# The beginning of a fused Fourier-mixing and feed-forward kernel: bit conversion without ScalarE, more buffers, spare PSUM banks, a shorter second chunk

## The chip, the cores and the metric

One Trainium2 chip; the program runs on one of its cores. The metric is the device time of one execution in microseconds (us), as a median of several executions. A profile is one more execution under the hardware profiler. TensorE multiplies matrices, VectorE and ScalarE do elementwise work, GpSimd does it too, slower here (a product of 128x512 elements took 1.30 us on it and 0.69 on VectorE), SP (SyncE) only issues DMAs. Runs whose time lies over 1.5% above the fastest of the same kernel count as slow.

## The reference

For x of (8, 3008, 256) the kernel computes a real FFT over the 3008 positions, multiplies by a complex filter, transforms back, and sends the 24064 resulting rows through a feed-forward block with a hard-swish:

```python
X = np.fft.rfft(x, axis=1)
F = (filt_r + 1j * filt_i)[None, :, :]
y = np.fft.irfft(X * F, n=x.shape[1], axis=1).astype(np.float32)
h = y.reshape(24064, 256) @ w_in            # (256, 2048), float64
g = h * np.clip(h + 3.0, 0.0, 6.0) / 6.0
out = (g @ w_out).astype(np.float32)        # (2048, 256), float64
```

The two weight matrices come as float64. The kernel has to turn their bits into float32 itself.

## The kernel before

The transform is split as 3008 = 47 x 64. For each batch: *first forward stage* (`a_unit`, eight units of four columns, results stored to z in DRAM), *second forward stage* (z loaded again, `b_unit` for 12 pairs of frequencies, filter product `f_unit` and `y_unit` on VectorE, inverse `bi_unit`, stored to g), *last stage* (`n_unit` on chunks of five of the 32 column groups, 94 tokens each). The main loop then runs the feed-forward block over 47 blocks of 512 tokens, eight items to a block. Batches 1 to 7 are transformed inside that loop; batch 0 has to be done ahead of it, and while that happens the weights are converted. That beginning is what the change is about.

```python
    def w_conv(i):                                    # 512 KB of float64 bits to float32
        ...
        v.tensor_scalar(out=big, in0=hi, ... shift left 3, and)
        v.scalar_tensor_tensor(out=big, in0=hi, scalar=top_c, in1=big, and, or)
        high = hi.bitcast(FP32)
        nc.scalar.activation(out=high, in_=high, func=AXT.Abs)
        v.tensor_scalar(out=rest, in0=big, ... exponent)
        v.tensor_scalar(out=lo, in0=lo, ... low bits as a fraction)
        v.scalar_tensor_tensor(out=rest, ...)         # low part
        v.scalar_tensor_tensor(out=rest, ...)         # plus high part
        v.tensor_scalar(out=high, in0=high, scalar1=SMALL, scalar2=None, op0=ALU.is_ge)
        nc.gpsimd.tensor_tensor(out=w_part(i)[1], in0=two(rest), in1=two(high), op=ALU.mult)
        # ... four sums or differences of 128x128 on GpSimd
    def a_unit(b, c):
        xc = xs[(b * NB + c) % 3]                     # three buffers for x
        t = t1p.tile(...)                             # two buffers
        ps = [psF.tile([P, 2, D], FP32, name="psf", tag="f") for h in range(2)]   # two banks
        # ... 4 matmuls, then two ScalarE evictions into t
    # the beginning of batch 0
        for c in range(3):
            x_load(0, c)
        w_load(0)
        w_load(1)
        for c in range(NB):                           # NB = 8
            a_unit(0, c)
            z_store(0, c, (nc.sync, nc.scalar))       # 2 DMAs on each queue
            if c + 3 < NB:
                x_load(0, c + 3)
            elif c + 3 == NB:
                table_load(0, 0)
            if c % 2:
                convert(1)
        # ... z loads and tables, then for i in range(NU + 1):  (NU = 12)
                b_unit(0, i); f_unit(0, i); y_unit(0, i)
                if i % 3 == 1:
                    convert(1)
                # ... bi_unit(0, i - 1), g_store, the next loads
        convert(2)
        # ... last-stage loads, n_unit for two chunks, main loop with the other six conversions
```

## Time and profile before

| | before |
|---|---|
| median | 2829.74 us (2827.22 to 2830.05) |
| span of the profiled run | 2827.1 us |
| first z load issued | 50.6 us |
| VectorE's first filter product | 58.4 us |
| its last y | ends at 121.9 us |
| first product of the main loop | 144.5 us |

The times of the table are starts and ends read in the timeline. TensorE is full from about 215 us to the end, so only the beginning can change, and in it the questions are which engine, queue or wait sets each of its stages. The prediction below shows the lines.

### The profile page before, as it was taken

What the parts mean: (1) busy time and instruction counts of PE and PEld (TensorE: products, weight loads), DVE (VectorE), ACT (ScalarE), POOL (GpSimd) and SP (SyncE); (2) the same over time, 40 slices, a digit from 0 to 9 for tenths busy, and PEclk for the clock granted to TensorE, in tenths of its full rate; (3) what the DMA queues carried; (4) which work ended last, traced back from release to release, by engine and by line L of the source; (5) the groups of instructions that cost most, each with busy time, mean ns of one, the idle gap of its engine ahead of it and who ended that gap; (6) DMA issues with size and microseconds to landing.
All of it is one profiled execution on the core that took longest, in us unless ns stands there. A gap on an engine that the chain in (4) does not pass through costs nothing.

```text
span 2827.1 us, 47246 instructions
## 1 busy us (share of the span) xinstructions
PE 2728.8 (97%) x18096; PEld 2467.2 (87%) x18096; DVE 1981.8 (70%) x3463; ACT 1340.4 (47%) x2686; POOL 411.1 (15%) x604
## 2 busy tenths in 40 slices
PE   4589999999999999999999999999999999999997
PEld 1369988999889998899989999899998999999996
DVE  4777875777657776577766777667775677766665
ACT  2144445444554445544455444544455444445443
POOL 3361012100120011201021101210012100000000
PEclk9799999999999999999999999999999999999998
DMA  7543213321233112322124221342113421100000
GB/s 211 174 128 111 78 55 100 94 64 53 76 84 103 57 60 71 93 84 81 40 81 112 62 66 42 87 115 76 48 47 90 112 66 47 40 26 24 17 8 16
DMA packets 127673, 211.89 MB, mean 75 GB/s; under 512 B 22232, under 2 KB 86360, under 8 KB 127448
## 3 DMA queue, kind: packets, MB, share of 16 engines
q1 hardware_dynamic: 104216, 151.69, 19.0%
q0 software_dynamic: 19104, 52.46, 6.4%
q10 hardware_dynamic: 4128, 4.72, 0.5%
q8 instruction: 143, 2.34, 0.3%
q14 instruction: 82, 0.67, 0.1%
HBM read 133.81 MB, written 74.97 MB: 74 GB/s over the span
## 4 chain that ended last, share of the span: by engine, by line
PE 92%; DVE 4%; DMA 2%; ACT 1%; issue 1%; POOL 0%; SPq 0%; POOLq 0%; ACTq 0%; DVEq 0%
PE po L418 41%; PE al L342 23%; PE be L342 17%; PE psn L317 4%; PE psf L261 3%; PE psf L289 3%; PE psf L236 2%; DMA z_tmp<-t 1%; DVE g L392 0%; DVE g L399 0%; DVE s L183 0%; DVE s L193 0%; DVE s L275 0%; DVE h L368 0%; DVE s L274 0%
## 5 line engine op out<-in xcount | busy, mean ns | idle before, releaser
L418 PEld LDWEIGHTS po<-w_out,g 128*128 128x128 f32 x10528 | 1401.8, 192 | 123.0 <-DVE g L400 30.4
L418 PE MATMUL po<-w_out,g 128*128 128x128 f32 x10528 | 1426.8, 276 | 4.6 <-DVE g L392 4.0
L392 DVE SCALAR_TENSOR_TENSOR g<-r,h 128x512 f32<-128x512 f32 x752 | 516.7, 687 | 256.5 <-ACT r L387 243.4
L387 ACT ACTIVATE r<-h,half_c 128x512 f32<-128x512 f32 x752 | 542.7, 722 | 321.1 <-DVE h L368 308.8
L342 PE MATMUL al<-xt,w_in 128*128 128x256 f32 x2256 | 676.1, 382 | 6.3 <-DVE h L373 4.7
L368 DVE TENSOR_TENSOR h<-be,s 128x512 f32<-128x512 f32 x376 | 259.6, 690 | 276.2 <-PE be L342 254.7
L342 PE MATMUL be<-xn,w_in 128*128 128x256 f32 x1504 | 447.8, 379 | 0.0
L342 PEld LDWEIGHTS al<-xt,w_in 128*128 128x128 f32 x2256 | 342.9, 192 | 9.7 <-DVE h L373 5.5
L382 ACT ACTIVATE h<-al 128x256 f32<-128x256 f32 x376 | 144.4, 384 | 373.6 <-PE al L342 373.6
L342 PEld LDWEIGHTS be<-xn,w_in 128*128 128x128 f32 x1504 | 286.1, 190 | 38.9
L373 DVE TENSOR_TENSOR h<-al,s 128x256 f32<-128x256 f32 x376 | 159.4, 424 | 191.6 <-PE al L342 191.2
L400 DVE TENSOR_TENSOR g<-g 128x512 f32<-128x512 f32 x376 | 261.4, 695 | 12.9
L363 ACT ACTIVATE s<-al 128x256 f32<-128x256 f32 x376 | 144.5, 384 | 202.0 <-PE al L342 202.0
L354 ACT ACTIVATE s<-be 128x256 f32<-128x256 f32 x376 | 144.4, 384 | 178.3 <-PE be L342 178.3
L342 PE MATMUL al<-xn,w_in 128*128 128x256 f32 x752 | 225.2, 381 | 0.5 <-ACT h L382 0.5
L342 PE MATMUL be<-xt,w_in 128*128 128x256 f32 x752 | 224.1, 380 | 0.0
L249 POOL DMA_DIRECT2D z_tmp<-t x224 | 132.5, 596 | 422.6 <-ACT t L239 419.5
L353 ACT ACTIVATE s<-al 128x256 f32<-128x256 f32 x376 | 144.4, 384 | 68.9 <-PE al L342 68.9
L399 DVE TENSOR_TENSOR g<-g 128x256 f32<-128x256 f32 x376 | 166.5, 443 | 12.8
L402 DVE TENSOR_TENSOR g<-g 128x256 f32<-128x256 f32 x376 | 165.0, 439 | 12.8
L342 PEld LDWEIGHTS be<-xt,w_in 128*128 128x128 f32 x752 | 143.2, 190 | 19.4
L317 PEld LDWEIGHTS psn<-wai,t 128*128 128x128 f32 x1024 | 135.4, 197 | 18.1 <-POOL w_out L202 12.5
(50 smaller groups left out, 1753.2 us busy)
## 6 DMA issues: line engine op xcount, KB each, us to landing
t<-z_tmp SPq DMA_DIRECT2D x48, 512.0 KB
t<-g_tmp SPq DMA_DIRECT2D x184, 120.0 KB
z_tmp<-t POOLq DMA_DIRECT2D x224, 96.0 KB, 2.8
g_tmp<-t POOLq DMA_DIRECT2D x42, 512.0 KB, 3.4
xs<-in_x_dram SPq DMA_DIRECT2D x128, 128.0 KB
out_dram<-o SPq DMA_DIRECT2D x328, 47.0 KB
ft<-in_filt_r_dram SPq DMA_DIRECT2D x96, 128.0 KB
ft<-in_filt_i_dram SPq DMA_DIRECT2D x96, 128.0 KB
```

The costliest lines, as they stand in the source:

```text
L317: nc.tensor.matmul(ps[:, ts(q, TOK)], t4[i % 2][:, q, ts(dh, P)], wai, start=True, stop=True)
L342: nc.tensor.matmul(ps, w_in[p][:, w, :], x, start=start, stop=stop, skip_group_check=True)
L353: nc.scalar.activation(out=s[:, 0, :], in_=al, func=AXT.Copy)
L363: nc.scalar.activation(out=s[:, 1, :], in_=al, func=AXT.Copy)
L368: nc.vector.tensor_tensor(out=st["h"][0].rearrange("p (a n) -> p a n", a=2), in0=be, in1=s, op=ALU.add)
L373: nc.vector.tensor_tensor(out=st["h"][1][:, 256:512], in0=al, in1=s5, op=ALU.add)
L387: nc.scalar.activation(out=r, in_=st["h"][i], func=AXT.Relu, bias=half_c, scale=1.0 / 6.0)
L392: nc.vector.scalar_tensor_tensor(out=st["g", k, p][:, o:o + 2, :].rearrange("p a n -> p (a n)"), in0=st["r", i], scalar=1.0, in1=st["h"][i ...
L399: v.tensor_tensor(out=g[:, G1, :], in0=g[:, G3, :], in1=g[:, G22, :], op=ALU.add)
L400: v.tensor_tensor(out=g[:, G3:G2 + 1:2, :], in0=g[:, G3:G1 + 1, :], in1=g[:, G11:G11 + 1, :].broadcast_to([P, 2, 256]), op=ALU.subtract)
L402: v.tensor_tensor(out=g[:, G4, :], in0=g[:, G12, :], in1=g[:, G2, :], op=ALU.subtract)
L418: nc.tensor.matmul(st["po", k][bank][:, part, u, :], g[:, a, ts(u, P)], w_out[p][:, w, :], start=(p == 0 and n in OPENS and u == 0), stop= ...
```

## The change

The intent: get batch 0 through its transform sooner. ScalarE's Abs leaves the conversion, so that evictions never queue behind a conversion, and the compare at its end moves from VectorE to GpSimd; six chunks of x have a place at once (three of them in `xn`, idle until the last stage) and are asked for on two queues; four tiles of bits instead of two can be in flight (two of them in the idle `g` buffers); six conversions stand beside the first stage; the forward stages of batch 0 use the four PSUM banks of the down product, idle until the main loop; and the second last-stage chunk has one column group instead of five, so that the main loop starts after six groups instead of ten.

```diff
     def w_load(i):
+        if i < 8 and i % 4 > 1:
+            t = gp.tile([P, 7, 256], FP32, name="g").bitcast(I32)[:, 0:4, :].rearrange(...)
+        else:
+            t = op.tile([P, 1024], I32, name="bits", tag="o")
...
-        high = hi.bitcast(FP32)
-        nc.scalar.activation(out=high, in_=high, func=AXT.Abs)
...
-        v.tensor_scalar(out=high, in0=high, scalar1=SMALL, scalar2=None, op0=ALU.is_ge)
+        v.tensor_scalar(out=hi, in0=hi, scalar1=20, scalar2=0x7FF,
+                        op0=ALU.logical_shift_right, op1=ALU.bitwise_and)
+        high = hi.bitcast(FP32)
+        nc.gpsimd.tensor_scalar(out=high, in0=hi, scalar1=897.0, scalar2=None, op0=ALU.is_ge)
         nc.gpsimd.tensor_tensor(out=w_part(i)[1], in0=two(rest), in1=two(high), op=ALU.mult)
...
+    def bank(b):
+        if b:
+            return psF.tile([P, 2, D], FP32, name="psf", tag="f")
+        st["bank"] = i = (st.get("bank", -1) + 1) % 4
+        return psO.tile([P, 2, 2, P], FP32, name="po%d" % i).rearrange("p a u m -> p a (u m)")
...
-    chunks = [(b, j, min(NJ, HC - j)) for b in range(B) for j in range(0, HC, NJ)]
+            n = 1 if b == 0 and j == NJ else min(NJ, HC - j)
...
-        for c in range(3):
-            x_load(0, c)
-        w_load(0)
-        w_load(1)
+        for c in range(6):
+            x_load(0, c, (nc.sync, nc.scalar)[c % 2])
...
+        convert(0)                    # loads every bits tile that has a free buffer
         for c in range(NB):
             a_unit(0, c)
             z_store(0, c, (nc.sync, nc.scalar))
-            if c + 3 < NB:
-                x_load(0, c + 3)
-            elif c + 3 == NB:
+            if c < 2:
+                x_load(0, c + 6)
+            if c == 2:
                 table_load(0, 0)
-            if c % 2:
-                convert(1)
+        convert(6)
...
-                if i % 3 == 1:
+                if i % 3 == 2 and i < NU - 1:
                     convert(1)
```

More of the change, by code (lines that the diff above doesn't have):

```diff
@@ L41 @@
 NJ = 5
-SMALL = float(np.array(897 << 20, np.int32).view(np.float32))
 RING = 3 * BLK
@@ L164, in w_part, with w_before @@
         return src.rearrange("(a p) d -> p a d", p=P), w_out[p][:, 0:4, :].rearrange("p (a j) m -> p a (j m)", a=2)
+    def w_before(i):
+        return i - 4 if i < 10 else i - 2
     def w_load(i):
-        if i >= NCONV:
-            return
-        t = op.tile([P, 1024], I32, name="bits", tag="o")
+        if i < 8 and i % 4 > 1:
+            t = gp.tile([P, 7, 256], FP32, name="g").bitcast(I32)[:, 0:4, :].rearrange("p a n -> p (a n)")
+        else:
+            t = op.tile([P, 1024], I32, name="bits", tag="o")
         nc.gpsimd.dma_start(t.rearrange("p (a d) -> p a d", a=2), w_part(i)[0])
@@ L173, in w_conv @@
     def w_conv(i):
-        if i >= NCONV:
-            return
         words = st.pop(("bits", i)).rearrange("p (n two) -> p n two", two=2)
@@ L217, with x_tile, x_load @@
     G11, G3, G1, G2, G4, G12, G22 = range(7)
-    def x_load(b, c):
-        t = xs[(b * NB + c) % 3]
+    def x_tile(b, c):
+        i = (b * NB + c) % 3
+        if b == 0 and 3 <= c < 6:
+            return xn.rearrange("p a n -> p (a n)")[:, ts(i, XC * D)].rearrange("p (j d) -> p j d", j=XC)
+        return xs[i]
+    def x_load(b, c, q=None):
+        q = q or nc.sync
+        t = x_tile(b, c)
         rows = x[b].rearrange("(a c) d -> a c d", c=NC)
@@ L225, in x_load @@
             for r, n in ((0, 32), (32, NA - 32)):
-                nc.sync.dma_start(t[h * 64 + r:h * 64 + r + n, :, :], rows[r:r + n, ds(h * HC + c * XC, XC), :])
+                q.dma_start(t[h * 64 + r:h * 64 + r + n, :, :], rows[r:r + n, ds(h * HC + c * XC, XC), :])
+    def bank(b):
[3 more added lines that the diff above has]
+        return psO.tile([P, 2, 2, P], FP32, name="po%d" % i).rearrange("p a u m -> p a (u m)")
     def a_unit(b, c):
-        xc = xs[(b * NB + c) % 3]
+        xc = x_tile(b, c)
         t = t1p.tile([P, 2, XC // 2, D], FP32, name="t1")
-        ps = [psF.tile([P, 2, D], FP32, name="psf", tag="f") for h in range(2)]
+        ps = [bank(b) for h in range(2)]
         for g in range(2):
@@ L258, in b_unit @@
         c, r = divmod(2 * i, TC)
-        ps = psF.tile([P, 2, D], FP32, name="psf", tag="f")
+        ps = bank(b)
         for u in range(2):
@@ L296, in g_store @@
         q.dma_start(g_d[b, ts(c, TC), :, :].rearrange("k p d -> p k d"), st.pop(("t3", b, c)))
-    chunks = [(b, j, min(NJ, HC - j)) for b in range(B) for j in range(0, HC, NJ)]
+    chunks = []
+    for b in range(B):
+        j = 0
+        while j < HC:
+            n = 1 if b == 0 and j == NJ else min(NJ, HC - j)
+            chunks.append((b, j, n))
+            j += n
     def token(i):
@@ L471 @@
     with tc.manual_schedule():
+        nc.sync.dma_start(wa, wa_d)
+        for t in xs[:2]:
+            nc.vector.memset(t, 0.0)
+        for t in xs[2], xn:
+            nc.gpsimd.memset(t, 0.0)
         nc.vector.memset(half_c, 0.5)
         nc.vector.memset(top_c, -0x40000000)
-        for i, t in enumerate(xs):
-            (nc.vector, nc.gpsimd, nc.vector)[i].memset(t, 0.0)
-        nc.sync.dma_start(wa, wa_d)
-        for c in range(3):
-            x_load(0, c)
-        w_load(0)
-        w_load(1)
-        done = 0
-        def convert(n):
-            nonlocal done
-            for _ in range(n):
-                w_conv(done)
-                w_load(done + 2)
-                done += 1
+        for c in range(6):
+            x_load(0, c, (nc.sync, nc.scalar)[c % 2])
+        loaded = done = 0
+        def convert(n):
+            nonlocal loaded, done
+            for i in range(n + 1):
+                while loaded < NCONV and w_before(loaded) < done:
+                    w_load(loaded)
+                    loaded += 1
+                if i < n:
+                    w_conv(done)
+                    done += 1
+        convert(0)
         for c in range(NB):
```

## The prediction

> **What bounds the kernel now.** I read the page first. Its slice rows say where time is left:
>
> ```profile
> PE   4589999999999999999999999999999999999997
> DVE  4777875777657776577766777667775677766665
> PEclk9799999999999999999999999999999999999998
> ...
> PE 92%; DVE 4%; DMA 2%; ACT 1%; issue 1%; POOL 0%; SPq 0%; POOLq 0%; ACTq 0%; DVEq 0%
> ```
>
> A slice is 70.7 us. From the fourth on TensorE is full to the end, and nothing in the diff touches that part except the cutting of batch 0 into last-stage chunks (same matmuls, one more chunk). PE is busy 2728.8 of 2827.1 us, so everything that is not PE work is 98 us, nearly all in the first 215 us, and it could not all be won: 2% of the time would be 57 us. So I cut the beginning into stages, by the busy-time view, at points found in the timeline: 0 to 50.6 the first forward stage (DFT over a, store of z); to 58.4 the first load of z until VectorE starts; to 121.9 the second forward stage, paced by unit; to 144.3 the tail (last g store, first last-stage matmuls); to 209.6 the seven items of the main loop that still hold conversions.
>
> ```profile
> core 0: us, PE busy (x) PEld busy (x) DVE busy (x) ACT busy (x) POOL busy (x), PEclk, DMA share, GB/s
> 0.00:50.60 50.60, 23.79 (x64) 4.84 (x64) 19.20 (x32) 12.61 (x21) 18.83 (x31) 1.00 0.69 197
> 50.60:58.40 7.80, 2.04 (x5) 1.70 (x6) 0.00 (x0) 0.00 (x0) 2.82 (x3) 1.00 0.84 257
> 58.40:121.90 63.50, 41.79 (x89) 25.07 (x87) 57.11 (x88) 8.80 (x15) 17.20 (x23) 0.85 0.60 180
> 121.90:144.30 22.40, 10.46 (x44) 9.62 (x44) 7.85 (x14) 3.62 (x6) 9.27 (x15) 0.50 0.74 194
> 144.30:209.60 65.30, 57.65 (x334) 42.33 (x333) 55.28 (x86) 30.89 (x63) 45.22 (x62) 0.95 0.44 126
> ```
>
> Stage one: no engine is half busy, and the DMA engines are at 0.69. The chain of waits of that stretch names what sets it (column: share of the chain): DMA of z, 48.9%.
>
> ```profile
> by line: DMA z_tmp<-t 48.9%; PE psf L236 13.0%; DMA xs<-in_x_dram 11.6%; DMA t<-z_tmp 10.0%; issue 4.9%; ACT t L239 4.2%; SPq L226 2.7%; DVE xs L479 1.6%; SPq L249 1.1%; ACTq L249 0.7%; DVE half_c L476 0.1%; SPq L254 0.1%; ACTq L239 0.1%; D
> ```
>
> Stage two: VectorE busy 57.11 of 63.50, so it is the bound. The remaining 6.4 us are short gaps. In the waits of 56 to 124 us two lines matter: VectorE waited for the second forward matmul 14.1 us, of which 11.4 are the stage's first load, so only 2.7 us within the stage; and the matmul of the inverse waited for ScalarE's eviction, because that eviction stood in ScalarE's order behind an Abs that waited for VectorE.
>
> ```profile
> ACT bits L187 <- DVE s L183: 34.4, 3, 20.3
> ...
> DVE s L273 <- PE psf L261: 14.1, 4, 11.4
> ...
> PE psf L289 <- ACT t L292: 9.1, 4, 2.8
> ```
>
> The tail: the timeline shows the last g store issued at 124.73, then
>
> ```profile
> 119.67 13.11 SPq L311 DMA_DIRECT2D t<-g_tmp  x16
> ...
> 135.89 8.82 PE L317 MATMUL psn<-wai,t 128*128 128x94 f32 x40 [11.82 <-POOL w_out L202]
> ```
>
> The reader is to see that these forty matmuls (20 in the program, two passes each) start when the last loads, which ended their issue at 132.8, can have landed; the wait is put down to GpSimd, but nothing these matmuls read comes from GpSimd's conversion, so I take it for the DMA. Each takes 0.22 us from start to start, at the half clock of that row.
>
> **What the Trainium skill says.** (1) "DMA: Bandwidth & Descriptors", Issuing engines are not separate DMA queues: DMAs of several issuers run on the same 16 engines and interleave, and a second issuer saves only issue time. The trace agrees in that sum: with all three issuers busy (50.6 to 58.4) the share is 0.84 at 257 GB/s. So x on ScalarE's queue is no new bandwidth. (2) "SBUF — State Buffer", SBUF: two separate sides: a VectorE instruction with two SBUF inputs contends with a GpSimd instruction that reads SBUF, and the loser blocks. The trace agrees: the 128x256 addition at L399 took 1.41 us beside the GpSimd multiply of a conversion, 0.443 us on average over the run. (3) "GPSIMD Engine Reference", Performance versus the Vector engine: at best 1.8 cycles per element, 769 ns for 512 elements. The new GpSimd compare is a one-input instruction of 512 elements, for which the trace before has no row; my estimate from that page is 0.8 to 1.1 us. (4) "PSUM — Partial Sum Buffer", The four PSUM rules: one matmul output lies within one 2 KiB bank; the forward tiles (512 fp32) fit the down product's banks exactly, and the down product does not start before the main loop, so these four banks are free.
>
> **The change part by part.**
>
> *Conversion.* VectorE has seven instructions before (L181 0.43, L183 0.75, L188 0.43, L190 0.42, L193 0.69, L195 0.69, L196 0.42, of the timeline: 3.8 us, some 4.2 with starts and collisions with GpSimd) and seven after: the float compare becomes an integer shift-and-mask of the same size. So no VectorE time is saved. Removed: ScalarE's Abs (0.67 us) and the two hand-overs VectorE to ScalarE to VectorE (18.0 us of VectorE waiting over the whole run, almost all in stage one, where VectorE has time). Added: about 1 us of GpSimd for each of 16 conversions, on top of 1.3 to 1.7 (multiply) plus 1.9 to 2.5 (four sums).
>
> *Where the conversions stand.* Before: 4 in stage one, 4 in stage two, 2 in the tail, 6 in the main loop. After: 6 before stage two's first filter (beside stage one, as VectorE has nothing else then), 3 in stage two (units 2, 5, 8), 2 in the tail, 5 in the main loop. More bits buffers let six be loaded in time: two tiles of the output pool plus two of g.
>
> *Stage one.* All x but two chunks is asked for at once, PSUM gives two units in flight instead of one, and Abs no longer stands in ScalarE's order. Against it: the bytes. x 3.1 MB, z 3.1, first tables 1.0 are as before, but about ten bits tiles of 0.5 MB are now wanted by the stage's end instead of some five to six, so 2 MB more on engines at 0.69 x 50.6 us. At full share (197 / 0.69 = 285 GB/s) the 10 MB of before need 35 us, and 12 MB need 42, plus 3 us until the first byte. Also t1 still has two buffers, so a unit still waits for the z store of two units earlier to land, and ScalarE's twelve x issues stand before its first eviction (before, 12 issues on the SP queue took 9.51 us, waiting on earlier landings): first eviction about 15 instead of 12 us. The z stores of ScalarE are 3.2 to 6.5 us apart now; the long ones had Abs or tables in between. I take 46.5 instead of 50.6: minus 4. The first load of z stays 7.8.
>
> *Stage two.* One conversion fewer, 4.2 us; of the 2.7 us of waiting for the matmul, caused by sharing two banks between forward and inverse, about 2 us go as the four banks let forward run ahead. Sum minus 6. Check: 12 units of five VectorE instructions (0.692 + 0.682 + 0.695 + 0.733 + 0.736, 3.54 plus starts, 3.6) are 43, three conversions 12.6, gaps 2: 57.6 against 63.5.
>
> *Tail.* Twelve matmuls of the last stage before the loop instead of twenty (six units of work, both halves): 16 x 0.22 = 3.5 us less. But the sums for the first block wait now for a short chunk with less cover; I give 0.5 back: minus 3. The path there (inverse, eviction, g store, loads, landing) does not touch the two conversions beside it.
>
> *Main loop.* Five items with a conversion instead of six. Seven items took 65.3 us, 9.3 each, against 14.4 for the two that follow, 7.2 each. PE idle in them is only 65.3 - 57.65 = 7.65 us, so one conversion fewer is worth 1.3 to 2.1. The GpSimd compare takes that back: VectorE's two-input sums stand beside one more microsecond of GpSimd, five times about 0.3. Minus 0.5.
>
> Sum: -4 - 6 - 3 - 0.5 = -13.5, so 2829.7 - 13.5 = 2816.2 us.
>
> **The rivals.** (a) Stage one is bound by bytes: ten bits tiles beside x and z keep z back, and stage one ends at 50 or later. For it: z is the chain now, and packets of the three queues interleave. Against: the share is only 0.69. Then the gain is 9 us: 2821. (b) GpSimd becomes the bound while converting: it was busy 45.2 of 65.3 in the converting items; with 1 us more, 5.5 of 9.3 per item, it does not fill, but it can hold VectorE for a whole instruction each time, 1 to 1.3 us per item. Then the loop loses 5 us: 2821 too, and with (a) 2826. (c) Everything joins well: evictions without Abs bring each g store and the next tables earlier, stage one ends at 42, forward running ahead keeps TensorE at the full clock (0.50 in the tail now) so that the tail's matmuls take half: another 10 us, 2806. (d) Stage two starved by tables: it needs 2 MB for two units (8.5 us, 235 GB/s), near what the queues gave; one wait for filter rows of 1.3 us is there already. Costs up to 5 us.
>
> **Range and chances.** Stage one carries plus or minus 5, stage two 3, tail 3, loop 3; added as independent, 7; I widen it for the PE clock: 2804 to 2826. All rivals lie within 2% of 2829.7 (2773 to 2886), as the whole beginning has not 57 us to give: faster by over 2% 0.01, within 0.98, slower 0.01.
>
> **What would show it.** Right: the last z store lands at 44 to 49 us; VectorE's first filter product at about 54, its last y at about 112; the last-stage matmuls before the loop x24 in about 5.3 us; the first product of the loop at about 131; then items of 9 to 9.5 us five times; PE full from about 195. Wrong: a first eviction after 20 us or a DMA share above 0.9 up to stage two's start (a); L399, L400 above 1.4 us in the loop (b); L273 waiting for filter rows or z (d); a tail at PE clock 1.00 (c).

## The result, and the profile after

The changed kernel takes 2822.96 us (2821.93 to 2824.12, four runs) against 2829.89 of before (four runs). The ratio is 0.9977, 95% interval 0.9960 to 0.9994. A ratio is the mean time of one kernel's fast runs over that of the other's of the same rounds, so it is not quite the ratio of the medians. About 7 us were won where 13.5 were forecast. The time lies inside the forecast range, but the gain is half of the predicted one, so the sum of steps has to be opened.

The changed kernel's slice rows and its chain's summary by engine show no other place than the beginning:

```profile
PE   4589999999999999999999999999999999999997
DVE  6787865777657776677756777567775677766665
PEclk7699999999999999999999999999999999999998
...
PE 92%; DMA 3%; DVE 2%; POOL 1%; issue 1%; ACT 0%; SPq 0%; ACTq 0%; POOLq 0%; DVEq 0%
```

The chain has less VectorE (2% instead of 4%) and more DMA (3% instead of 2%). The same busy-time view as in the prediction, cut at the same events of the changed kernel (columns as there):

```profile
core 0: us, PE busy (x) PEld busy (x) DVE busy (x) ACT busy (x) POOL busy (x), PEclk, DMA share, GB/s
0.00:54.40 54.40, 19.25 (x64) 4.34 (x64) 34.01 (x46) 9.97 (x17) 45.02 (x54) 0.76 0.77 224
54.40:60.60 6.20, 2.09 (x5) 1.75 (x6) 0.01 (x1) 0.00 (x0) 0.83 (x1) 0.50 0.95 300
60.60:118.50 57.90, 32.36 (x88) 22.35 (x87) 54.80 (x81) 6.57 (x11) 16.57 (x19) 0.75 0.58 175
118.50:133.10 14.60, 6.08 (x26) 5.45 (x26) 9.35 (x15) 1.64 (x4) 10.02 (x11) 0.55 0.55 163
133.10:194.50 61.40, 51.23 (x286) 37.06 (x287) 48.61 (x73) 24.46 (x51) 46.02 (x61) 0.91 0.52 140
```

The first stage is now longer than before, 54.4 us instead of 50.6, the second and the tail are shorter. Adding up between events of the two timelines:

| stretch | before | after | change | predicted |
|---|---|---|---|---|
| start to VectorE's first filter product | 58.44 | 60.59 | +2.2 | -4 |
| to the end of its last y | 63.4 | 58.0 | -5.5 | -6 |
| to the loop's first product | 22.6 | 15.2 | -7.4 | -3 |
| main loop to the end | 2682.6 | 2686.3 | +3.7 | -0.5 |
| sum (span of the profiled runs) | 2827.1 | 2820.1 | -7.0 | -13.5 |

The chain of waits of the first 60 us says what sets the first stage in the changed kernel (shares of that chain), and the view of DMA queues of each kernel's first stage says how much was moved in it (packets, MB, share; q0 is GpSimd's queue, which in this stretch carries only bits). First the chain, then the queues of the changed kernel to 54.4 us, then those of the kernel before to 50.6:

```profile
by line: DMA z_tmp<-t 42.1%; DMA xn<-in_x_dram 23.6%; DMA ft<-in_filt_i_dram 9.2%; ACT t L255 7.8%; DMA xs<-in_x_dram 5.2%; issue 3.2%; DVE xs L500 3.0%; ACTq L265 2.8%; SPq L270 1.6%; SPq L140 1.5%; SPq L265 1.0%; SPq L142 0.7%; ACTq L235 
```

```profile
DMA packets 5313, 12.21 MB, mean 224 GB/s; under 512 B 1136, under 2 KB 1520, under 8 KB 5310
...
q0 software_dynamic: 1326, 4.84, 31.4%
```

```profile
DMA packets 4704, 9.97 MB, mean 197 GB/s; under 512 B 1072, under 2 KB 1456, under 8 KB 4704
...
q0 software_dynamic: 720, 2.62, 19.8%
```

Nearly all of the added 2.24 MB are bits (4.84 - 2.62 = 2.22). The second thing that stands out is the start of the stage. The issue row of ScalarE's queue and its first eviction in the changed kernel, then the first eviction in the kernel before:

```profile
6.24 11.65 ACTq L235 DMA_DIRECT2D xn<-in_x_dram  x8
...
19.21 1.08 ACT L255 ACTIVATE t<-po 128x512 f32<-128x512 f32 x2
20.33 0.75 ACTq L265 DMA_DIRECT2D z_tmp<-t  x2
```

```profile
11.96 1.08 ACT L239 ACTIVATE t<-psf 128x512 f32<-128x512 f32 x2 [9.94 <-PE psf L236]
13.07 0.91 ACTq L249 DMA_DIRECT2D z_tmp<-t  x2
```

ScalarE spent 11.65 us issuing eight loads of x, because the issues themselves waited: the trace's records show the DMAs of the SP and ScalarE queues sharing eight completion semaphores, and each load waiting for the landing of the one that used its semaphore last. So the first z store came 7.3 us later than before. Two explanations of the first stage therefore stood against each other: the late start, or the bytes. The experiments take them first.

### The profile page after: what moved, and what is told of

Read it like the earlier page. It is cut to its first block, busy times and chain, and to the rows that moved or that the text cites. A ratio compares the mean times of both kernels' runs of the same rounds, so it can differ in the third digit from the quotient of the medians.

```text
span 2820.1 us, 47236 instructions
## 1 busy us (share of the span) xinstructions
PE 2713.0 (96%) x18096; PEld 2461.9 (87%) x18096; DVE 1991.3 (71%) x3463; ACT 1329.8 (47%) x2672; POOL 437.3 (16%) x621
## 4 chain that ended last, share of the span: by engine, by line
PE 92%; DMA 3%; DVE 2%; POOL 1%; issue 1%; ACT 0%; SPq 0%; ACTq 0%; POOLq 0%; DVEq 0%
PE po L440 41%; PE al L364 23%; PE be L364 17%; PE psn L339 4%; PE psf L305 3%; PE psf L277 3%; PE psf L252 2%; DMA z_tmp<-t 1%; DMA xn<-in_x_dram 1%; DMA ft<-in_filt_i_dram 0%; DMA xs<-in_x_dram 0%; DVE y L296 0%; ACT t L255 0%; DVE y L297 0%; DVE s L291 0%
## 5 line engine op out<-in xcount | busy, mean ns | idle before, releaser
L424 DVE TENSOR_TENSOR g<-g 128x256 f32<-128x256 f32 x376 | 168.8, 449 | 12.8
L364 PEld LDWEIGHTS be<-xt,w_in 128*128 128x128 f32 x752 | 143.0, 190 | 20.8 <-POOL xt L357 1.6
L357 POOL TENSOR_TENSOR xt<-xn 128x256 f32<-128x256 f32 x94 | 71.4, 759 | 495.0 <-ACT xn L345 495.0
```

Source lines behind the costliest of these rows:

```text
L364: nc.tensor.matmul(ps, w_in[p][:, w, :], x, start=start, stop=stop, skip_group_check=True)
L424: v.tensor_tensor(out=g[:, G4, :], in0=g[:, G12, :], in1=g[:, G2, :], op=ALU.subtract)
```

## The experiments

All are edits of the changed kernel, and all gave correct results. Their first-stage reading is the time at which the first load of z is issued, because that load waits for the last z store; 54.5 us in the changed kernel. Each series of experiments had its own runs of the kernel before, whose medians lie between 2827.33 and 2829.89 us. So a difference of 1 to 3 us between totals of different series is within the noise, and where it matters the text gives it by the ratios to before as well.

### All early x on the SP queue

```diff
-            x_load(0, c, (nc.sync, nc.scalar)[c % 2])
+            x_load(0, c)
```

> The changed kernel with all six early x chunks asked for on the SP queue, so ScalarE's queue holds no loads ahead of its first eviction. In the changed kernel the first eviction is at 19.2 us, the first z store at 20.3, the first load of z at 54.5. Theory A (place in the order: each DMA of the two hardware queues is issued only when the one eight places before it has landed, so 24 loads placed ahead of the first store hold it back whoever issues them): first eviction back at about 12, but the first z store stays at 17 or later, first load of z at 52 to 54.5, total within 2 us of 2823. Theory B (issuer: the loads only stand in ScalarE's way): first z store at about 13, first load of z at 47 to 48, total about 2816. Theory C (bytes: ten tiles of bits beside x and z): first load of z unchanged at 54 to 55, total unchanged.

2823.77 us (2822.02 to 2824.84). First load of z at 55.25. ScalarE in its timeline:

```profile
8.02 1.08 ACT L255 ACTIVATE t<-po 128x512 f32<-128x512 f32 x2 [6.01 <-PE po L252]
9.13 0.97 ACTq L265 DMA_DIRECT2D z_tmp<-t  x2
...
27.09 1.08 ACT L255 ACTIVATE t<-po 128x512 f32<-128x512 f32 x2 [14.07 <-DMA z_tmp<-t]
```

The first eviction and ScalarE's half of the first store are 11 us earlier, and nothing comes of it: the third unit then waits 14.07 us for the stores of z to give its t1 buffer back, as their other half stands on the SP queue behind the loads. The first stores on that queue, in the changed kernel and here:

```profile
20.48 0.74 SPq L265 DMA_DIRECT2D z_tmp<-t  x2
```

```profile
21.34 0.73 SPq L265 DMA_DIRECT2D z_tmp<-t  x2
```

Theory B falls. Theory A's number for the first store (17 or later) was wrong for ScalarE's half of it and right for SP's. That the end stays where it was is what theory C said, but with SP's half as late as in the changed kernel this run does not tell A from C.

### x three chunks ahead, as before the change

```diff
-        for c in range(6):
-            x_load(0, c, (nc.sync, nc.scalar)[c % 2])
+        for c in range(3):
+            x_load(0, c)
...
-            if c < 2:
-                x_load(0, c + 6)
+            if c + 3 < NB:
+                x_load(0, c + 3)
```

> The changed kernel with x asked for as before the change: three chunks at the start, then chunk c+3 after unit c, all on the SP queue; bits, banks and conversion stay changed. Theory A: first z store at about 13 us, first load of z at 47 to 50, total 2816 to 2819. Theory B: the same as with all x on the SP queue. Theory C: the first z store is earlier, but the first load of z stays at 53 to 55 and the total within 2 us of 2823.

2824.69 us (2823.81 to 2826.92). ScalarE's half of the first z store at 9.13 us, SP's at 16.30, first load of z at 55.41. Theory A's 47 to 50 did not come. But this is not the whole order of before: the first tables stay where the change put them, behind unit 2 and not behind unit 5, and the last load of x was issued only at 42.0 us (28.3 in the changed kernel). The early start held for five units (the fifth was evicted from 29.3 us, 35.0 in the changed kernel) and was lost at the sixth (40.2 and 42.5). So an early start that is undisturbed is not tested by this run.

### Only four tiles of bits early

```diff
-                while loaded < NCONV and w_before(loaded) < done:
+                while loaded < NCONV and w_before(loaded) < done and (loaded < 4 or st.get("go")):
...
-        convert(6)
+        convert(4)
...
+        st["go"] = True
+        for i in range(4, 8):
+            w_load(i, nc.sync)
+        loaded = 8
...
-        convert(2)
+        convert(4)
```

> The changed kernel with only four tiles of bits loaded and four conversions done beside the first stage (3 MB fewer asked for there); the other two conversions go to the tail, so the total isn't the reading, the first stage is. Theory C: first load of z at 46 to 49 instead of 54.5. Theory A and B: the first z store comes a little earlier (18 to 20 instead of 20.3), as the loads ahead of it land sooner, and the first load of z at 51 to 54. The total is expected to be 2825 to 2832, as the tail gets 8 us of VectorE more.

The other four of the first eight tiles are asked for after the first loads of z and tables. First load of z at 47.58, with the first z store still at 20.88. That load, and the queues of its first 47.6 us:

```profile
47.58 0.94 SPq L270 DMA_DIRECT2D t<-z_tmp  x2
...
DMA packets 4561, 9.45 MB, mean 199 GB/s; under 512 B 1056, under 2 KB 1440, under 8 KB 4560
...
q0 software_dynamic: 576, 2.10, 15.6%
```

With 2.74 MB of bits fewer the stage is 6.9 us shorter, 2.5 us for each MB, although it starts as late as in the changed kernel. In the chain of the first 60 us the waits for stores of z fell from 42.1% to 27.6%. This is what theory C said, but two conversions were taken out of the stage as well; the runs with held bits below keep all six. (The total, 2830.99 in its one run of unknown state, pays for two conversions more in the tail: from the first product of item 0 to that of item 1 it took 26 us.)

### The select on VectorE

The compare of GpSimd and its multiply become one VectorE instruction, which writes the weights:

```diff
-        high = hi.bitcast(FP32)
-        nc.gpsimd.tensor_scalar(out=high, in0=hi, scalar1=897.0, scalar2=None, op0=ALU.is_ge)
-        nc.gpsimd.tensor_tensor(out=w_part(i)[1], in0=two(rest), in1=two(high), op=ALU.mult)
+        v.scalar_tensor_tensor(out=w_part(i)[1], in0=two(hi), scalar=897.0, in1=two(rest),
+                               op0=ALU.is_ge, op1=ALU.mult)
```

> The changed kernel with GpSimd's compare (1.8 us) and multiply (1.3 us) of a conversion made one VectorE instruction (compare, then multiply; 0.7 us), which also writes the weights; GpSimd keeps the four sums. Theory L (the 3.7 us lost in the main loop are GpSimd's compare, which holds VectorE's two-input sums and delays GpSimd's z issues and block sums): items 0 to 5, 61.7 us from the first product to that of item 6 in the changed kernel against 58.3 before, become 54 to 58, total 2815 to 2820. Rival M (VectorE's own work is the bound in these items): 0.7 us more for each conversion, items as long or longer, total 2822 to 2827.

2817.19 us (2815.90 to 2818.82), ratio to before 0.9960 (0.9944 to 0.9977). From the first product of item 0 to that of item 6: 55.9 us instead of 61.7. Theory L holds and rival M falls, although VectorE has an instruction of 0.69 us more. The lines of GpSimd and VectorE around one conversion in the changed kernel, in order of time, show why:

```profile
147.35 1.94 POOL L198 TENSOR_SCALAR bits<-bits 128x512 f32<-128x512 int32 x1 [9.51 <-DVE bits L195]
149.38 1.30 POOL L200 TENSOR_TENSOR w_out<-s,bits 128x512 f32<-128x512 f32 x1
```

```profile
147.89 0.74 DVE L421 TENSOR_TENSOR g<-g 128x256 f32<-128x256 f32 x1
148.67 0.69 DVE L422 TENSOR_TENSOR g<-g 128x512 f32<-128x512 f32 x1
149.39 1.57 DVE L424 TENSOR_TENSOR g<-g 128x256 f32<-128x256 f32 x1
```

L424 is a two-input instruction that takes 0.42 us when alone; it begins with GpSimd's two-input multiply and ends after it. The compare itself takes 1.94 us here, not 0.8 to 1.1.

### The old form of the conversion in the loop only

```diff
+        if i >= 11:
+            nc.scalar.activation(out=hi.bitcast(FP32), in_=hi.bitcast(FP32), func=AXT.Abs)
...
+        if i < 11:
+            # ... the changed form
+        else:
+            v.tensor_scalar(out=high, in0=high, scalar1=SMALL, scalar2=None, op0=ALU.is_ge)
```

> The changed kernel, but the five conversions of the main loop in the form before the change (absolute value on ScalarE, float compare on VectorE, multiply on GpSimd). Theory L (GpSimd's new compare made the loop's items longer): from the first product of item 0 to that of item 6 57 to 59 us instead of 61.7, total 2819 to 2821. Rival M (the items are longer for another reason, such as the shorter cover for the first block's sums): 61 to 62 us, total 2822 to 2824.

2821.04 us (2819.18 to 2822.90), items 0 to 5 in 59.9 us. So 1.8 of the 3.7 us lost in the loop are the compare in the loop's conversions; the reading lies 0.9 above what theory L said. Item 0 stays at 10.4 us (10.0 in the changed kernel, 7.8 before): the two conversions of the tail keep the compare in this edit, and the next experiment shows the other half of the cause. In this profile the first load of z was at 58.6, with the same program up to there as in the changed kernel: the first stage differs by some us between executions.

### First chunks of five units again

```diff
-            n = 1 if b == 0 and j == NJ else min(NJ, HC - j)
+            n = min(NJ, HC - j)
```

> The changed kernel with the first two last-stage chunks of five units each again. In the changed kernel the last-stage matmuls start 10.2 us after VectorE's last y of the second stage began, and the loop's first product comes 5.7 us after that. Theory P (as predicted: only eight of the twenty matmuls were saved): start unchanged at 10.2, first product 3 to 4 us later, total +2.5 to +3.5. Theory Q (the loads ahead of them, 0.96 MB instead of 0.58, also held the start back): start 12.5 to 14.5 us after the last y, first product 5.5 to 7.5 us later, total +5 to +7.

2825.54 us (2824.10 to 2826.83), so the shorter chunk is worth 2.6 by the medians and 3.7 by the ratios to before (0.9990 and 0.9977). The last-stage matmuls in the timelines of the changed kernel and of this one:

```profile
128.03 4.98 PE L339 MATMUL psn<-wai,t 128*128 128x94 f32 x22 [8.23 <-DMA t<-g_tmp]
```

```profile
131.32 8.82 PE L339 MATMUL psn<-wai,t 128*128 128x94 f32 x40 [10.05 <-DMA t<-g_tmp]
```

Counted from the start of the last y (117.86 and 118.78), they begin 2.4 us later, and the loop's first product follows after 8.6 us instead of 5.7. That is theory Q, 5.2 us (its range began at 5.5), but the total moves by half of it only. In these two profiles item 0 takes 3.2 us back (6.8 with the long chunk, 10.0 with the short one) and the loop from item 6 to the end 0.8.

In item 0 TensorE waits for the block sums of GpSimd (`t_sums`, four differences that a block's products need): 1.6 us for weights, 0.8 for matmuls, by the waits of that stretch. With the long chunk the last-stage matmuls are still running meanwhile and cover them. GpSimd is late because of the conversions of the tail: in the changed kernel it works without a gap from 122.5 us, through both conversions, to the first block sum at 134.9, which is 1.2 us after the loop's first product. In the run with the select on VectorE the first block sum starts 0.3 us before that product, and item 0 takes 7.8 us although the chunk is short. So both are needed for the loss, the short cover and the compare and multiply of the tail's conversions.

The eight matmuls that the short chunk leaves out are done later in the full loop. At items 14 and 15 the changed kernel has a chunk of five that the kernel before doesn't have there, and each is 1.1 us longer (8.1 instead of 7.0), 0.22 for a matmul: by that, eight would be 1.8 us. But item 12 is 1.2 us shorter (7.5 instead of 8.7), which is why no more than 0.8 is seen.

### Forward stages in the two shared banks again

```diff
-        if b:
+        if True:
             return psF.tile([P, 2, D], FP32, name="psf", tag="f")
```

> The changed kernel with the forward stages back in the two shared PSUM banks. In the changed kernel VectorE's first filter product and the last one are 54.4 us apart. As predicted, the banks save 2 us of waits in the second stage: 56 to 57 us apart with two, and nothing in the first stage, which is bound by bytes (first load of z at 54 to 55): total +1 to +3, 2824 to 2826. Rival: with the ScalarE stalls gone two banks are enough, 54.4 to 55 us, total unchanged.

2827.56 us (2825.03 to 2829.09). VectorE's first and last filter product are 56.3 us apart instead of 54.4, so the banks are worth the 2 us that were predicted for the second stage, and nothing before it (first load of z at 54.8). The total is 4.6 up (5.1 by the ratios to before). The profiled run was the fastest of this kernel, its span 3.1 above that of the changed kernel: 1.9 in the second stage, 1.0 before the first filter product, where one profile of each can't tell it from chance. What the slower runs have on top isn't seen in any profile, and with runs that spread over 4 us I leave it there.

### Bits tiles 6 to 9 held back

Six conversions stay beside the first stage; the tiles that only later conversions need are asked for on the SP queue after the first loads of z and tables. On the version with the select on VectorE:

```diff
-                while loaded < NCONV and w_before(loaded) < done:
+                while loaded < NCONV and w_before(loaded) < done and (loaded < 6 or loaded > 9):
...
+        for loaded in 6, 7:
+            w_load(loaded, nc.sync)
...
                         table_load(0, c + TB)
+                        if c < 2:
+                            w_load(8 + c, nc.sync)
+                            loaded = 9 + c
```

> The version with the compare and multiply in one VectorE instruction (2817.2 us), and with the loads of bits tiles 6 to 9 held back until the first loads of z and the first tables are asked for (2 MB fewer beside the first stage, still six conversions there). Theory C (bytes bind the first stage; four conversions' bits fewer gave 6.9 us for 3 MB): first load of z at 50 to 52 instead of 55.6, total 2812 to 2814. Rival N (the bytes only move: 2 MB beside the first tables hold the second stage's start or its tables back by as much): the first load of z is earlier but the first filter product isn't, or VectorE waits for filter rows; total 2816 to 2819.

2813.63 us (2813.23 to 2814.17). First load of z at 52.1 instead of 55.6, first filter product at 58.1 instead of 61.7. The first load of z in the version without this edit and in this one:

```profile
55.64 0.94 SPq L268 DMA_DIRECT2D t<-z_tmp  x2
```

```profile
52.08 0.94 SPq L268 DMA_DIRECT2D t<-z_tmp  x2
```

Theory C holds, rival N falls: the bytes found room in the second stage.

The same edit on the changed kernel itself:

> The changed kernel itself with the loads of bits tiles 6 to 9 held back until the first loads of z and the first tables are asked for; nothing else. Theory C (the first-stage term failed for these bytes): the first load of z at 50 to 52 instead of 54.5, the first filter product at 56 to 58 instead of 60.6, the second stage as long as before (54.4 us from first to last filter product), total 2818 to 2821 instead of 2823. Rival (in the changed kernel GpSimd's longer conversions or the late first store set the stage's end): first load of z at 53.5 to 55, total within 1 us of 2823.

2819.17 us (2818.96 to 2822.19), 3.8 less than the changed kernel by the medians, 1.7 by the ratios to before (0.9971 and 0.9977), so the gain in the total isn't clear of the noise. First load of z in the changed kernel and here:

```profile
54.45 0.94 SPq L270 DMA_DIRECT2D t<-z_tmp  x2
```

```profile
52.88 0.94 SPq L270 DMA_DIRECT2D t<-z_tmp  x2
```

First load of z at 52.9 and first filter product at 58.9, both 0.9 outside what theory C said but on its side; the second stage as long as before the edit (54.1 us from first to last filter product). Half of the gain of these two profiles is later: item 0 took 8.4 us instead of 10.0. The difference at the first load of z alone could be chance (58.6 and 54.5 were read for one and the same beginning); what carries it is that all runs with held bits lie below all without, in the table further down.

### The last conversion two items later

```diff
         for i in range(NCONV - done):
-            at(i, convert, 1)
+            at(i if i < 4 else i + 2, convert, 1)
```

> The version with the select on VectorE and the bits held back (2813.6 us), with the last conversion moved from item 4 to item 6, so that it doesn't meet the four block sums of GpSimd. In that version item 5 (175.2 to 188.8) takes 13.6 us, its neighbours 9.2, and VectorE's conversion instructions in it take 0.84 to 1.10 us instead of 0.42 to 0.75. Theory L (GpSimd holds VectorE): items 5 to 7 together, 28.3 us now, become 24 to 26; total 2810 to 2812. Rival (the item is long for the late z issues on GpSimd's queue, which come anyway): 27 to 29 us, total 2813 to 2814.

2810.12 us (2808.85 to 2814.14), ratio to before 0.9939 (0.9927 to 0.9951). Items 5 to 7 take 25.5 us instead of 28.3; the total is 3.5 lower by the medians, 2.3 by the ratios. Theory L again: in the version without this edit the conversion met GpSimd's block sums, as VectorE's and GpSimd's lines of that version show:

```profile
177.44 0.91 POOL L355 TENSOR_TENSOR xt<-xn 128x256 f32<-128x256 f32 x1
178.31 0.91 POOL L355 TENSOR_TENSOR xt<-xn,xt 128x256 f32<-128x256 f32 x1
```

```profile
177.68 0.95 DVE L189 TENSOR_SCALAR bits<-bits 128x512 int32<-128x512 int32 x1
178.66 1.10 DVE L192 SCALAR_TENSOR_TENSOR s<-bits,s 128x512 f32<-128x512 f32 x1
```

The same two instructions take 0.43 and 0.69 us where GpSimd is idle. This is the fastest version.

### The same with all early x on the SP queue

> The same, with all six early x chunks on the SP queue: the first z store is then at about 9 us instead of 20. Theory C, bytes still bind the first stage with 2 MB fewer: first load of z within 1 us of 52, total within 1.5 us of the version without. Rival: with fewer bytes the late first store is the bound now: first load of z at 46 to 50, total 2 to 5 us less.

2810.21 us (2808.80 to 2810.61): no difference, with ScalarE's half of the first z store at 9.1 us. First load of z at 51.7 (49.7 in the one profile without it). So with 1.7 MB fewer, too, it is worth nothing to take the loads off ScalarE's queue. As in the first experiment SP's half of the first store stays late (21.8 us; 20.8 without the edit), so this isn't a test of a stage that starts early as a whole.

### Five conversions early, three in the tail

```diff
-        convert(6)
+        convert(5)
...
-        convert(2)
+        convert(3)
```

(with the bits buffers moved along)

> The version with the last conversion later, with five conversions beside the first stage instead of six and three in the tail instead of two. Theory C: half a megabyte fewer is worth 0.8 to 1.2 us at the first load of z (about 51), and VectorE is idle in the tail, so the first product of the loop keeps its distance of about 15.4 us from the last y; total 1 us less. Rival: the third conversion of the tail isn't done when item 0 needs VectorE or the weights: item 0 and 1 longer, total 1 to 5 us more.

2812.88 us (2811.27 to 2815.24), 2.8 more. First load of z at 50.4, so no gain there that could be told from the spread; the first product of the loop came 16.2 us after the last y began instead of 15.6, and item 0 took 10.3 us instead of 7.9. The rival holds: a third conversion in the tail isn't free.

## Why the prediction was wrong

**Stage one: the step that failed.** The prediction had the bytes right (12 MB; 12.21 were moved) and named the bytes as its rival (a), but its sum gave the added 2 MB no cost of their own: it divided all bytes by a rate, "At full share (197 / 0.69 = 285 GB/s)", and took the 42 us that came out as covered by the stage. The share went from 0.69 only to 0.77 and the mean rate to 224 GB/s. A DMA share under one was read as room. It wasn't free: z goes through two t1 buffers, so each unit waits for the landing of an earlier store, and with 2.74 MB of bits fewer these waits shrank and the stage was 2.5 us shorter for each MB. That single stores land later because bits share the engines with them is the likely reason; no view here shows it for one store. The readings of the changed kernel and all its edits sort by the bits:

| bits in or asked for before the first load of z | first load of z |
|---|---|
| four tiles (2.1 MB) | 47.6 |
| five tiles, one kernel | 50.4 |
| six tiles (3.1 MB), four kernels | 49.7 to 52.9 |
| about ten tiles (4.8 MB in the changed kernel), seven kernels | 54.5 to 58.6 |

In the six-tile row the fastest version (49.7), the one with x on SP (51.7), the held bits with the select (52.1) and on the changed kernel (52.9) stand together. All four lie below all seven with about ten tiles, and two of them differ from a run of the other row by the held bits alone (52.1 and 55.6, 52.9 and 54.5). Runs of one program differ by up to 4.1 us (54.5 and 58.6), so no single pair would show it.

Predicted 46.5 for the stage's end, measured 54.4; up to the first filter product predicted -4, measured +2.2, which is 6.2 of the 6.5 us by which the sum missed.

The late first eviction, which the prediction had put at 15 us, came at 19.2. Taking the loads off ScalarE's queue did not win it back, but no run starts both halves of the stores early with the rest unchanged, so what the late start costs by itself isn't shown. The signs that the prediction gave for (a), an eviction after 20 us or a share above 0.9, did not appear although the stage ended after 50: the sign was set too high, by the same reading of the share. Rival (b), GpSimd holding the loop, came true as well in part (3.7 us lost; it said 5).

**Stage two: right.** -6 predicted, -5.5 measured; 1.9 us for the banks, measured alone, which leaves 3.6 for the conversion that is no longer there (4.2 predicted, not measured alone).

**Tail and loop: the sum right, both terms wrong.** -3.5 predicted for the two, -3.7 measured, as -7.4 and +3.7: that the sum fits is luck. In the tail I counted matmuls only, and these gave 2.9 us (8.6 to 5.7). The smaller loads ahead of them gave 2.4 more. The other 2 us aren't explained: with long chunks, too, the matmuls start 12.5 us after the last y in the changed form and 14.8 before, and no run takes that apart. In the loop the prediction said that nothing in the diff touched the full part but "same matmuls, one more chunk", and expected 0.5 to be won. Items 0 to 5 took 3.4 us more. Item 0 lost 2.2, for the missing cover and GpSimd's conversions. In items 1 to 5 the conversion that left gave 1.0 (50.5 us before, 49.5 with the old form in the loop), and the compare took 2.2 (51.8; over items 0 to 5 it is 1.8, as item 0 differed by 0.4). Of the 5.2 us that the short chunk wins in the tail, about half reaches the total.

**The compare on GpSimd.** Estimated at 0.8 to 1.1 us and at 0.3 us of VectorE's time for each conversion; it took 1.94 in the loop (1.54 at its shortest). Taken back in the loop it gives 1.8 us. With compare and multiply off GpSimd everywhere, items 0 to 5 are 5.8 us shorter, 2.2 of them in item 0.

**Slips of reading in the prediction.** None of them decides the result. That "all three issuers" were "busy (50.6 to 58.4)" isn't so: in that stretch the SP queue and GpSimd's queue moved packets (1.47 and 0.52 MB), ScalarE's none. "5.5 of 9.3 per item" for GpSimd should be 7.5: 45.2 of 65.3 us are 6.5 for each of seven items before the added 1 us. The seven items end at 211.1 us and not at 209.6, so they took 66.6 us.

**What stays open.** What the late first store costs by itself; the 2 us of the tail above; why the total rises by 4.6 with two banks when the stage they serve gives 1.9; and how much of a difference of 1 to 2 us at the end of the first stage is chance, as every kernel has one profile only.

## What to carry to other kernels

A DMA share under one (0.69 here) isn't free room for prefetch when the transfers that the chain waits for are on the same engines: ask what must land next, and hold back what isn't needed until that has landed. Work or cover that is taken out of one stage can be missing in the next (here 5.2 us won in the tail, 3.2 of them lost in item 0), so count it there. An instruction moved to GpSimd can cost VectorE too while both run (1.57 us instead of 0.42 for a two-input sum; 0.95 instead of 0.43 for L189, which has one input); here it was cheaper to give VectorE one instruction more and GpSimd two fewer.

## What the Trainium skill lacked or had wrong

- "GPSIMD Engine Reference", Performance versus the Vector engine: its best case of 769 ns for 512 elements misled the estimate. A one-input compare of 512 int32 elements to float32, at a stride of two words, took 1.54 to 2.18 us in these traces; the page's one figure for strided reads is for strides over 8 bytes, this stride is 8 bytes, and it has none for an instruction that converts.
- "DMA: Bandwidth & Descriptors", Issuing engines are not separate DMA queues: the runs agree (2810.12 with x on two queues, 2810.21 on one). No page read here says what else a second issuer costs: the two queues shared eight completion semaphores in this program, and ScalarE was held for 11.65 us by eight issues.
- The same page gives a fixed and a variable cost of one DMA, but no rate for a mix of loads and stores with waits between them: the first stage moved 197 to 224 GB/s at shares of 0.69 to 0.77, and the stretch after it, with loads only, 300 GB/s at 0.95.
